# Sparse attention followed by a gated MLP: v on partitions 32 to 95, two raw buffers for k and q, halo rows moved by SyncE, and a new listed order

## The chip, the cores and the metric

The kernel runs on one core of one Trainium2 chip. The metric is the device time of one execution in microseconds. Three runs of the kernel before took 233.87, 235.32 and 235.61 us; their median is 235.32 us. One further execution was profiled; the profile tells the time of every instruction and transfer of that one. The engines are TensorE (PE, with its weight loads PEld), VectorE (DVE), ScalarE (ACT), GpSimd (POOL) and SyncE (SP), which here only starts transfers.

## What is computed

Four batches of eight heads, 768 positions, head size 64, and an MLP from 512 to 2048 and back on the 4 x 768 = 3072 tokens:

```python
# attention, per batch and head: 24 blocks of 32 positions
k_sum = k.reshape(B, H, nb, 32, D).max(axis=3)
v_sum = v.reshape(B, H, nb, 32, D).mean(axis=3)
local = where(abs(i - j) < 16, scale * q @ k.T, -1e9)      # 768 keys, a band of 31
coarse = scale * q @ k_sum.T + log(32)                     # 24 keys
a = softmax(concat([local, coarse], axis=-1))
x = a @ concat([v, v_sum], axis=2)                         # -> [3072, 512] over the heads
# MLP
h = x @ w_in
g = h * clip(h + 3.0, 0.0, 6.0) / 6.0
out = g @ w_out                                            # float32
```

## The kernel before, in words

**Tiles of the attention.** Queries are taken in 12 tiles of 64 (`QB`) per batch, shifted by 16 against the keys. Each tile sees a window of 96 keys (`WIN`: its own block of 64 keys and 32 of the next) and the 24 block maxima, so 120 rows (`KEYS`). `kaug` holds, for each of the four pairs of heads, these 120 key columns of every tile; `vaug` holds the 120 rows of v: window rows on partitions 0 to 95, block sums on 96 to 119, with a column of ones (32 for the sums) that yields the softmax's denominator. A score step (`scores`, names s...) is 24 small matmuls per pair of heads into a pair of PSUM banks, one exponential on ScalarE per half of the tiles (L527), and a multiplication by the 0/1 band on VectorE (L531). A value step (`values`, v...) is 16 or 32 matmuls (L632), a normalisation on VectorE, four transposes (L682) and a copy into x.

**How q, k and v arrive.** All loads from DRAM are started by GpSimd and turn float32 into bfloat16 on the way; they go through one queue in the order of their issue. Batch 0 loads k and q in natural rows (`knat`, `qnat`), and TensorE transposes them. Batches 1 to 3 load k and q raw (`load_raw`): 32 positions on 32 partitions, for one half of the head size and four heads, 3072 rows of 64 bytes; VectorE turns them in 32 x 32 blocks (`turn`, w..., L588 for k and L592 for q). There is one `kraw` and one `qraw`. A load of k takes one transfer per group of 32 partitions (L367), a load of q two, of 16 partitions each (L375), because of the shift by 16. v is loaded in four pieces (L385) onto partitions 0 to 63. The other 32 window rows, those of the next block, are copied inside the core for batch 0 (`halo`); for batches 1 to 3 they are a third load from DRAM (`load_vhalo`, L393, 380 KB), followed by a small move on SyncE for the last tile (L395). The block sums of v are a chain of small matmuls with the indicator `ind` over the 64 rows (L552 and L567); they are copied to the tiles on ScalarE and VectorE, for batches 2 and 3 by SyncE (L575).

**MLP.** The tokens come in eight half batches s = 0 to 7 of 384. Fsc (c = 0 to 3) is a quarter of the first product: per 128 hidden units four matmuls (L700), a ReLU on ScalarE (L705) and a gating step on VectorE that writes g (L707). Gst (t = 0 to 2) is the second product for 128 tokens (four groups of four matmuls of 512 columns, L720), a copy out of PSUM (L432, the line of the helper that records every copy) and a store by SyncE (L730, and L732 for the rows that wrap around the batch). The last tile is cut into two halves of 256 columns.

**What sets the order.** Nothing is reordered at run time. The string `ORDER` lists every operation with its number within its group (F00.3, w21.0, ...), and `:A` or `:D` says which of ScalarE and VectorE takes a copy. `Plan.run` walks the string and assigns buffers: three PSUM banks `h`, one `o`, two pairs `S`, three g, four x. Each engine then executes its own instructions in the order in which they were issued, and waits at one whose inputs are not there; what stands behind it waits too. A load is started in GpSimd's order, once its target is free. At the start some matmuls on constants (`keep`, L803) run between TensorE's first steps.

Of the kernel before, what the change touches and what calls it, by code (L numbers as in the profile page):

```python
# [21 lines left out]
VW = 66  # L22
# [19 lines left out]
F10.3 F12.1 F10.2 F12.2 F10.6 F10.4 F10.9 F10.5 F10.7 F10.8 F11.0 F10.10 F10.11 F11.6 F11.1 F11.9 F11.2 F11.7 F11.8 F11.10
F11.11 F12.6 F12.7 F12.8 F12.9 F12.10 F12.11 w12.0 G01.1 F13.0 F13.1 w13.0 F13.2 w11.0 w13.3 w10.0 w12.3 G01.2 G01.3 F12.3
F13.9 G01.4:A G02.0 G02.1 G02.2 G02.3 F11.3 F13.10 w11.2:A F12.4 F12.5 G02.4:A w12.2:A F13.3 F11.4 F13.4 w10.2:A w13.2:A
w12.4 w11.3 w11.4 w11.1 w11.5:D G00.0 G00.1 s110.0 s110.1 s110.3 w12.1 w13.1 w12.5:D w13.5:A G00.2 G00.3 s120.0 s120.1
s120.3 w13.4 w10.1 F13.5 w10.3 F11.5 w10.4 w10.5:D F13.11 V10.0 V13.0 V11.0 V23.0 V12.0 H1.0 K20.0 K22.0 V20.0 K21.0 Q231.0
K23.0 Q220.0 V22.0 V21.0 Q200.0 Q221.0 Q201.0 Q211.0 Q210.0 Q230.0 s130.0 G00.4:A F13.6 G12.0 s130.3 s130.1 F13.7 G00.5
G01.5 H1.1 G02.5 s120.2 s110.2 s130.2 s100.0 s100.1 F13.8 s100.2 s110.4 s100.3 G12.1 u1.0 u1.1:A u1.3:A u1.5:A G12.2 G12.3
G12.4:A u1.4:D u1.2:D v10.0 s120.4 v10.1 v10.5 v10.6 v10.2 s100.4 u1.7:A u1.6:A u1.9:A G11.0 G11.1 v12.0 v10.3 v10.4:A
u1.8:A v12.1 v12.2 s130.4 G11.2 v10.7 v12.3 v10.8:D G11.3 v12.4:A v13.0 F20.0 F20.3 G11.4:A F20.1 F20.4 v13.5 v13.1 v13.2  # L50
v13.6 F20.9 v13.3 v15.0 F20.10 F20.2 F20.5 F20.11 v15.1 v15.2 F20.6 F21.0 F20.7 F20.8 F21.1 V30.0 V31.0 V32.0 V33.0 F21.2
w21.0 F21.6 G10.0 F21.7 v13.4:A F21.8 F21.3 v15.3 v13.7 F21.9 F22.3 F21.4 F21.5 w20.0 F22.0 G10.1 F21.10 F22.4 v15.4:A
F21.11 F22.1 F22.5 F22.9 F23.0 F22.2 w20.3 F22.10 F22.11 F23.1 w21.2:A v13.8:A F23.2 w22.0 F22.6 u2.0 F22.7 F22.8 w21.3
# [796 lines left out]
```

## Time and profile before

| what | us |
|---|---|
| runs (three), median | 233.87, 235.32, 235.61; 235.32 |
| profiled execution, and its span from first to last instruction | 233.64; 231.9 |
| TensorE busy | 217.3 |
| VectorE busy | 156.7 |
| ScalarE busy | 126.5 |
| GpSimd busy | 72.8 |
| matmuls of the MLP's first product (L700), second product (L720) | 95.0; 82.3 and 10.9 |

The 1.7 us between the profiled execution's time and its span lie before the first and after the last instruction. A row that begins with a line number gives an engine, an operation, its output and its inputs with shapes and how often it occurred, then after a bar the busy time and the mean nanoseconds of one, and after another bar the idle time of the engine just before these instructions with what ended it. In the timeline the first two numbers are the start and the length; the bracket at the end is the idle time before it and what ended that.

### The profile page before, as it was taken

What the parts mean: (1) busy time and instruction counts of PE and PEld (TensorE: products, weight loads), DVE (VectorE), ACT (ScalarE), POOL (GpSimd) and SP (SyncE); (2) the same over time, 40 slices, a digit from 0 to 9 for tenths busy, and PEclk for the clock granted to TensorE, in tenths of its full rate; (3) what the DMA queues carried; (4) which work ended last, traced back from release to release, by engine and by line L of the source; (5) the groups of instructions that cost most, each with busy time, mean ns of one, the idle gap of its engine ahead of it and who ended that gap; (6) DMA issues with size and microseconds to landing.
All of it is one profiled execution on the core that took longest, in us unless ns stands there. A gap on an engine that the chain in (4) does not pass through costs nothing.

```text
span 231.9 us, 5321 instructions
## 1 busy us (share of the span) xinstructions
PE 217.3 (94%) x2175; PEld 121.8 (52%) x2175; DVE 156.7 (68%) x327; ACT 126.5 (55%) x258; POOL 72.8 (31%) x86
## 2 busy tenths in 40 slices
PE   7899699999989997989999889999999999999991
PEld 2365476555445563545565445555555555555560
DVE  2489689789897669889785499945955645454201
ACT  2287567774588854768654535675552543434101
POOL 7994481357754734707741200000000000000000
PEclk9999979999999999999999999999999999999998
DMA  5999999999999999999999990132002030012013
GB/s 76 169 123 182 191 206 196 119 77 87 95 120 176 186 103 86 85 114 146 84 142 89 127 71 0 45 80 84 3 11 85 0 136 3 0 45 90 3 68 114
DMA packets 126585, 22.14 MB, mean 95 GB/s; under 512 B 116960, under 2 KB 123616, under 8 KB 126560
## 3 DMA queue, kind: packets, MB, share of 16 engines
q0 software_dynamic: 117280, 14.81, 217.7%
q1 hardware_dynamic: 9280, 6.98, 12.7%
q8 instruction: 17, 0.28, 0.7%
q14 instruction: 8, 0.07, 0.1%
HBM read 29.60 MB, written 6.29 MB: 155 GB/s over the span
## 4 chain that ended last, share of the span: by engine, by line
PE 58%; DMA 18%; issue 9%; POOL 9%; ACT 2%; DVE 2%; DVEq 0%; POOLq 0%
PE h L700 26%; PE o L720 22%; DMA kraw<-in_k_dram 13%; DMA qnat<-in_q_dram 5%; PE h L720 4%; POOL vaug L385 3%; ACT at L527 2%; PE S L519 1%; PE S L632 1%; POOL qraw L375 1%; POOL qnat L357 1%; PE S L682 1%; POOL knat L346 1%; POOL win L417 1%; POOL kraw L367 1%
## 5 line engine op out<-in xcount | busy, mean ns | idle before, releaser
L700 PE MATMUL h<-x,win 128*128 128x384 bf16 (+1 forms) x536 | 95.0, 321 | 3.1 <-DVE g L707 3.1
L705 ACT ACTIVATE r<-h 128x384 f32<-128x384 f32 x128 | 60.4, 493 | 59.4 <-PE h L700 58.7
L707 DVE SCALAR_TENSOR_TENSOR g<-r,h 128x384 bf16<-128x384 f32 x128 | 67.5, 545 | 33.9 <-ACT r L705 32.1
L720 PE MATMUL o<-wout,g 128*128 128x512 bf16 x336 | 82.3, 379 | 0.2 <-ACT ot L432 0.2
L700 PEld LDWEIGHTS <-win 128*128 128x128 bf16 x536 | 49.9, 99 | 37.5 <-issue 3.6
L720 PEld LDWEIGHTS <-g 128*128 128x128 bf16 x400 | 38.1, 98 | 36.3
L375 POOL DMA_DIRECT2D qraw<-in_q_dram x24 | 21.3, 890 | 29.1 <-issue 10.5
L527 ACT ACTIVATE at<-S 120x768 bf16<-120x768 f32 x32 | 24.8, 812 | 7.1 <-PE S L519 7.1
L367 POOL DMA_DIRECT2D kraw<-in_k_dram x12 | 15.8, 1317 | 13.5 <-issue 12.0
L385 POOL DMA_DIRECT2D vaug<-in_v_dram x16 | 15.1, 949 | 4.8 <-PE h L700 3.1
L592 DVE STREAM_TRANSPOSE qaug<-qraw 128x800 bf16<-128x800 bf16 x12 | 11.8, 998 | 6.2 <-DMA kraw<-in_k_dram 3.3
L667 DVE TENSOR_TENSOR xn<-S,rc 128x512 bf16<-128x512 f32 (+1 forms) x25 | 15.7, 643 | 0.4
L531 DVE TENSOR_TENSOR at<-at,mask 96x768 bf16<-96x768 bf16 x28 | 14.8, 546 | 1.5 <-ACT at L527 1.0
L432 ACT COPY ot<-o 128x512 f32<-128x512 f32 x16 | 9.4, 586 | 11.3 <-PE o L720 10.6
L588 DVE STREAM_TRANSPOSE kaug<-kraw 128x768 bf16<-128x768 bf16 x12 | 11.5, 965 | 2.1 <-DMA kraw<-in_k_dram 2.1
L432 ACT COPY x<-S 128x512 bf16<-128x512 bf16 x19 | 11.0, 587 | 2.5 <-PE S L682 2.1
L519 PEld LDWEIGHTS <-kaug 64*128 64x128 bf16 x384 | 7.0, 96 | 8.2 <-issue 6.3
L605 DVE TENSOR_REDUCE red<-kaug 128x24 bf16<-128x768 bf16 x12 | 11.2, 940 | 0.0
L519 PE MATMUL S<-qaug,kaug 64*128 64x64 bf16 x384 | 9.2, 192 | 2.0 <-ACT at L527 1.2
L803 PE MATMUL o<-idle 128*128 128x512 bf16 x30 | 9.5, 442 | 1.5 <-DVE idle L287 1.5
L720 PE MATMUL h<-wout,g 128*128 128x512 bf16 (+1 forms) x64 | 10.9, 326 | 0.0
L632 PEld LDWEIGHTS <-at 120*64 120x64 bf16 x384 | 7.6, 111 | 5.9 <-issue 4.8
(84 smaller groups left out, 139.3 us busy)
## 6 DMA issues: line engine op xcount, KB each, us to landing
out_dram<-ot SPq DMA_DIRECT2D x19, 256.0 KB
vaug<-in_v_dram POOLq DMA_DIRECT2D x16, 192.0 KB, 10.7
kraw<-in_k_dram POOLq DMA_DIRECT2D x12, 192.0 KB, 14.8
qraw<-in_q_dram POOLq DMA_DIRECT2D x24, 96.0 KB, 11.9
win<-in_moe_w_in_dram POOLq DMA_DIRECT2D x4, 512.0 KB, 11.8
wout<-in_moe_w_out_dram POOLq DMA_DIRECT2D x4, 512.0 KB, 13.5
vaug<-in_v_dram POOLq DMA_DIRECT2D x3, 380.0 KB, 16.2
out_dram<-ot SPq DMA_DIRECT2D x4, 224.0 KB
```

Source lines behind the costliest of these rows:

```text
L367: op("POOL", 0.8, lambda hs=hs, ds=ds, rows=rows: nc.gpsimd.dma_start(out=kraw[rows], in_=k[b, hs].rearrange("h (c r) d -> r (h c) d", r=B ...
L375: nc.gpsimd.dma_start(out=qraw[lo:lo + PAD, 1 - x:1 - x + NP * NB], in_=src[PAD * (1 - x):PAD * (2 - x)])
L385: op("POOL", 0.95, lambda: nc.gpsimd.dma_start(out=o[0:QB, lo:hi, 0:D], in_=rows[:, lo:hi]), w=[("v", b % 2, c)], prio=prio, dma=1.7)
L432: {"ACT": nc.scalar.copy, "DVE": nc.vector.tensor_copy, "POOL": nc.gpsimd.tensor_copy}[eng](o, i)
L519: nc.tensor.matmul(X[p, half].slot[:, j, i * QB:(i + 1) * QB], kaug[p][rows, t], qT[rows, p, t * QB:(t + 1) * QB], start=not masked, stop= ...
L527: op("ACT", act(2 * HALF), lambda a=a, x=x: nc.scalar.activation(a, x.slot[0:KEYS, :, 0:HALF], AF.Exp, scale=scl), r=[x], w=[("at", p, hal ...
L531: op("DVE", dve(2 * HALF, 1.92), lambda m=m, half=half: nc.vector.tensor_tensor(m, m, mask[:, half * HQ:(half + 1) * HQ].unsqueeze(1).to_b ...
L667: nc.vector.tensor_tensor(o, src[..., 0:D], r.unsqueeze(len(r.shape)).to_broadcast(list(o.shape)), op=ALU.mult)
L700: nc.tensor.matmul(h.slot[:, lo * 128:hi * 128], w_in_sb[:, kt, ft * 128:(ft + 1) * 128], xt[s].slot[:, kt, lo * 128:hi * 128], start=(kt ...
L705: op("ACT", act(HALF), lambda: nc.scalar.activation(r.slot[:], h.slot[:, 0:HALF], AF.Relu, bias=0.5, scale=1.0 / 6.0), r=[h], w=[r], prio= ...
L707: op("DVE", dve(HALF), lambda: nc.vector.scalar_tensor_tensor(gt[s].slot[:, ft], r.slot[:], 1.0, h.slot[:, 0:HALF], op0=ALU.min, op1=ALU.m ...
L720: nc.tensor.matmul(o.slot[:, a:z], gt[s].slot[:, ft, ts * 128:(ts + 1) * 128], w_out_sb[:, ft, a:z], start=(ft == 0), stop=(ft == NFT - 1))
```

## The change

- **Place of v.** v is loaded onto partitions 32 to 95. The 32 further window rows lie on partitions 0 to 31 and hold the end of the previous block, so a tile's window is [32 keys of the previous block, its own 64]; the shift by 16 goes the other way, and the last block is the one before the first. Of each batch the second half of the tiles (6 to 11) is now treated first (`low`). Stores follow: the tile that wraps has its 16 wrapped rows first. The row of `vaug` is 80 wide in place of 66.
- **Halo rows.** The third load from DRAM is gone. Batch 1 copies them on ScalarE (five) and VectorE (three); batches 2 and 3 have one SyncE transfer inside the core of 3040 rows each and a small one of 256 rows.
- **Block sums** are taken over 96 rows, with zeros in the indicator and in the 32 rows that the halo will fill (`empty`: four memsets on VectorE at the start for one buffer, four on GpSimd for the other). For batch 0 the sums go to `vf`; for two pairs of heads the values of the first half take the sums' part by separate matmuls on `vf`, in place of two copies to the tiles.
- **Raw k and q** have two buffers each; the second pair shares its space with batch 0's natural k and q. A raw q load is one transfer of 32 partitions like one of k: 12 of them in place of 24. VectorE's block transpose of q is 768 wide in place of 800.
- **Batch 0's q**, second half, is loaded as three pieces of 128 positions (`qwide`), transposed by three matmuls per pair in place of eight.
- **Order.** A new `ORDER`: batch 1's loads come as k, v, q in place of k, q, v; the block maxima may be copied by ScalarE; the list ends with the copy (ScalarE) and store of 256 columns of the tile that is cut in two, in place of a copy of 512 columns and the two stores of a tile that wraps. Matmuls on constants at the start: 35 in place of 47. The constants with which the list was made (`SLOW`, `KRAW`, `LAT`, `room`) change, too.

```diff
@@ class Plan, and the buffers
-KRAW = 2.0
+KRAW = 1.6
...
-    qaug = sb([128, NP, BLK + S], BF16, "qaug")
-    qT = qaug[:, :, BLK:]
-    kraw = sb([128, NP * NB, BLK], BF16, "kraw")
-    qraw = sb([128, NP * NB + 1, BLK], BF16, "qraw")
+    qT = sb([128, NP, PAD + S], BF16, "qT")
+    first = sb([128, 2 * NP * NB, BLK], BF16, "first")
+    kraw, qraw = ([sb([128, NP * NB, BLK], BF16, f"{n}raw"), first[:, i * NP * NB:(i + 1) * NP * NB]] for i, n in enumerate("kq"))
...
-    knat = sb([RP, H, RUN, D], BF16, "knat")
-    qnat = [sb([RP, H, RUN // 2, D], BF16, f"qnat{i}") for i in range(2)]
+    knat, qnat = (first[0:RP].rearrange("p c x -> p (c x)")[:, lo:lo + H * n * D].rearrange("p (h s d) -> p h s d", h=H, s=n)
+                  for lo, n in ((0, RUN), (H * RUN * D, RUN // 2)))
+    qwide = sb([128, NS // 2, d_model], BF16, "qwide")
+    vf = [sb([128, 2, D + 2], BF16, f"vf{c}") for c in range(NP)]
...
-    ind = sb([QB, NQ, 32], BF16, "ind")
+    ind = sb([WIN, NQ, 32], BF16, "ind")
@@ const_ops
+        def empty(eng, i, c):
+            eng.memset(vaug[i][0:BLK, 2 * c:2 * c + 2, :, 0:D].bitcast(F32), 0.0)
+            if i == 0:
+                eng.memset(vf[c][WIN:KEYS, :, D:D + 2], float(BLK))
...
+    def low(x):
+        return (1 - x) * HQ
@@ load_raw
-            for x in range(2):
-                plan.at(f"Q{b}{g}{x}")
-                def go(x=x, hs=hs, ds=ds, lo=BLK * g + PAD * x):
-                    src = q[b, hs].rearrange("h (c r) d -> r (h c) d", r=BLK)[:, :, ds]
-                    nc.gpsimd.dma_start(out=qraw[lo:lo + PAD, 1 - x:1 - x + NP * NB], in_=src[PAD * (1 - x):PAD * (2 - x)])
...
+        for name, src, o in (("K", k, kraw[(b + 1) % 2]), ("Q", q, qraw[(b + 1) % 2])):
+            for g in range(4):
...
+                op("POOL", 1.32, lambda src=src, o=o, hs=hs, ds=ds, rows=rows: nc.gpsimd.dma_start(
+                    out=o[rows], in_=src[b, hs].rearrange("h (c r) d -> r (h c) d", r=BLK)[:, :, ds]),
...
@@ load_v, halo, halos
-        op("POOL", 0.95, lambda: nc.gpsimd.dma_start(out=o[0:QB, lo:hi, 0:D], in_=rows[:, lo:hi]),
+        op("POOL", 0.95, lambda: nc.gpsimd.dma_start(out=o[BLK:WIN, lo:hi, 0:D], in_=rows[:, lo:hi]),
...
-        op("POOL", 0.75, lambda: nc.gpsimd.dma_start(out=o[QB:WIN, 0:n - 1, 0:D], in_=rows[0:WIN - QB, 1:n]),
...
+        def go(eng):
+            copy(eng, o[0:BLK, hs, a:z, 0:D], o[QB:WIN, hs, a - 1:z - 1, 0:D])
+            if x:
+                copy(eng, o[0:BLK, hs, 0, 0:D], o[QB:WIN, hs, NQ - 1, 0:D])
...
+        op("SP", 0.7, lambda: nc.sync.dma_start(out=o[0:BLK, 1:n, 0:D], in_=o[QB:WIN, 0:n - 1, 0:D]),
+           r=[("v", i, c) for c in range(NP)], w=every, free=[("vz", i, c) for c in range(NP)], prio=prio, dma=3.4)
+        op("SP", 0.7, lambda: nc.sync.dma_start(out=end[0:BLK, :, 0, 0:D], in_=end[QB:WIN, :, NQ - 1, 0:D]),
...
@@ turn
-            out=w[:, :, 0:QB].rearrange("p t (n c) -> p t n c", n=2),
-            in_=kraw[:, p * NB:(p + 1) * NB].rearrange("p (t n) c -> p t n c", n=2)),
+            out=w[:, :, BLK:WIN].rearrange("p t (n c) -> p t n c", n=2),
+            in_=kraw[(b + 1) % 2][:, p * NB:(p + 1) * NB].rearrange("p (t n) c -> p t n c", n=2)),
...
-            out=qaug[:, p].rearrange("p (c x) -> p c x", x=BLK), in_=qraw[:, p * NB:(p + 1) * NB + 1]),
+            out=qT[:, p, PAD:PAD + S].rearrange("p (c x) -> p c x", x=BLK), in_=qraw[(b + 1) % 2][:, p * NB:(p + 1) * NB]),
@@ f2
-                nc.sync.dma_start(out=out[b * S + row:b * S + row + n, a:z], in_=ot.slot[0:n, a:z])
-                if n < 128:
-                    nc.sync.dma_start(out=out[b * S:b * S + 128 - n, a:z], in_=ot.slot[n:128, a:z])
+                if n:
+                    nc.sync.dma_start(out=out[(b + 1) * S - n:(b + 1) * S, a:z], in_=ot.slot[0:n, a:z])
+                nc.sync.dma_start(out=out[b * S + row + n:b * S + row + 128, a:z], in_=ot.slot[n:128, a:z])
```

Batch 1's part of the two lists, loads only:

```diff
-K10.0 K11.0 K13.0 K12.0 ... Q121.0 Q101.0 Q110.0 Q100.0 Q120.0 Q131.0 Q130.0 Q111.0 ... V10.0 V13.0 V11.0 V23.0 V12.0 H1.0
+K11.0 K12.0 O3.0 K13.0 z1.1:P K10.0 V12.0 V10.0 V13.0 ... Q10.0 V11.0 z2.1:P Q12.0 Q13.0 Q11.0
```

438 lines of the change are left out of this document (231 added, 207 removed).

## The prediction

> **What bounds the kernel now.** I read the first part of the page (how full each engine is), then its part 4 (the chain that ended last), then stretches of the span, to see where the fullest engine isn't full.
>
> ```profile
> span 231.9 us, 5321 instructions
> PE 217.3 (94%) x2175; PEld 121.8 (52%) x2175; DVE 156.7 (68%) x327; ACT 126.5 (55%) x258; POOL 72.8 (31%) x86
> PE 58%; DMA 18%; issue 9%; POOL 9%; ACT 2%; DVE 2%; DVEq 0%; POOLq 0%
> ```
>
> TensorE is the bound on average, but nearly a fifth of the chain is DMA. The stretches, cut where the batches change (columns: length, then PE, PEld, DVE, ACT, POOL busy with their instructions, granted clock, DMA share, GB/s):
>
> ```profile
> 60.00:80.00 20.00, 18.75 (x300) 10.20 (x299) 15.53 (x34) 17.39 (x31) 11.30 (x11) 1.00 3.75 150
> 80.00:100.00 20.00, 18.41 (x168) 10.47 (x167) 15.77 (x29) 11.35 (x27) 9.73 (x11) 1.00 5.71 96
> 100.00:140.00 40.00, 37.70 (x431) 21.25 (x431) 31.66 (x63) 23.96 (x51) 13.65 (x13) 1.00 3.63 108
> 140.00:227.30 87.30, 87.28 (x663) 47.50 (x661) 47.80 (x97) 38.59 (x81) 0.00 (x0) 1.00 0.13 43
> ```
>
> From 140 us to the end of the matmuls PE is full; nothing but less work helps there. What can be won lies before: 20 − 18.41 = 1.59 us idle between 80 and 100, 40 − 37.70 = 2.30 between 100 and 140, together 3.9. The chain (start, length) and the timeline name the holders:
>
> ```profile
> 14.98 12.10 DMA qnat<-in_q_dram
> 73.13 13.78 DMA kraw<-in_k_dram
> 107.74 10.84 DMA kraw<-in_k_dram
> 126.44 6.13 DMA kraw<-in_k_dram
> 227.37 0.69 DVE ot L432
> ```
> ```profile
> 87.10 0.98 DVE L588 STREAM_TRANSPOSE kaug<-kraw 128x768 bf16<-128x768 bf16 x1 [2.05 <-DMA kraw<-in_k_dram]
> 88.57 1.46 PE L700 MATMUL h<-x,win 128*128 128x384 bf16 x8 [1.37 <-DVE g L707]
> 132.64 1.01 DVE L592 STREAM_TRANSPOSE qaug<-qraw 128x800 bf16<-128x800 bf16 x1 [3.30 <-DMA kraw<-in_k_dram]
> 134.14 2.11 PE L700 MATMUL h<-x,win 128*128 128x384 bf16 x12 [1.73 <-DVE g L707]
> ```
>
> DVE stands in its list at the transpose of a raw k or q that hasn't landed (2.05 us, 3.30 us); the gating step g queued behind it is late, so PE idles 1.37 and 1.73 us. Those two are 3.1 of the 3.9. They have one cause: there is a single raw buffer, so the next batch's load can be issued only when the last transpose of this batch has read it.
>
> **The rates of the loads.** All loads go through GpSimd's software queue, and after the weights it is never empty, so batch 1's time is set by the sum of transfers. Four stretches of the queue, in this order: raw k alone; raw k and q mixed; v; weights; and a fifth of natural q and v at the start:
>
> ```profile
> DMA packets 6748, 0.44 MB, mean 118 GB/s; under 512 B 6747, under 2 KB 6747, under 8 KB 6747
> ...
> DMA packets 6374, 0.40 MB, mean 75 GB/s; under 512 B 6374, under 2 KB 6374, under 8 KB 6374
> ...
> DMA packets 5937, 0.75 MB, mean 117 GB/s; under 512 B 5937, under 2 KB 5937, under 8 KB 5937
> ...
> DMA packets 3455, 2.43 MB, mean 202 GB/s; under 512 B 1176, under 2 KB 3453, under 8 KB 3453
> ...
> DMA packets 840, 0.11 MB, mean 153 GB/s; under 512 B 840, under 2 KB 840, under 8 KB 840
> ```
>
> They last 3.7, 5.4, 6.4, 12 and 0.7 us. A raw load is 3072 packets of 64 B: 6748/3.7 = 1824 a us make 1.7 us a load, 6374/5.4 = 1180 make 2.6. A v load is 1536 packets of 128 B on partitions 0 to 63: 5937/6.4 = 928 a us, 1.66 us. The first rows of the batches need what has to land:
>
> ```profile
> 27.19 1.48 POOL L423 DMA_DIRECT2D wout<-in_moe_w_out_dram  x2 [2.24 <-DMA qnat<-in_q_dram]
> ...
> wout<-in_moe_w_out_dram POOLq DMA_DIRECT2D x1, 512.0 KB, 14.9
> ```
> ```profile
> 61.88 1.01 DVE L592 STREAM_TRANSPOSE qaug<-qraw 128x800 bf16<-128x800 bf16 x1 [1.05 <-DMA qraw<-in_q_dram]
> 63.30 0.52 PE L519 MATMUL S<-qaug,kaug 64*128 64x64 bf16 x24
> 73.48 0.83 PE L632 MATMUL S<-vaug,at 120*64 120x65 bf16 x32
> ```
>
> The second of the two last weight loads is issued at 27.19 + 0.74 = 27.9 and lands 14.9 later, at 42.8. Raw q of batch 1 is complete when its transpose starts, 61.9. The values product of batch 1 (v10.0 in the listed order) starts at 73.48.
>
> **The change part by part.** Durations used (the last number before the second bar is the mean ns):
>
> ```profile
> L527 ACT ACTIVATE at<-S 120x768 bf16<-120x768 f32 x32 | 24.8, 812 | 7.1 <-PE S L519 7.1
> L531 DVE TENSOR_TENSOR at<-at,mask 96x768 bf16<-96x768 bf16 x28 | 14.8, 546 | 1.5 <-ACT at L527 1.0
> L432 ACT COPY ot<-o 128x512 f32<-128x512 f32 x16 | 9.4, 586 | 11.3 <-PE o L720 10.6
> L432 ACT COPY kaug<-kaug 128x352 bf16<-128x352 bf16 (+1 forms) x22 | 6.5, 356 | 0.0
> L432 ACT COPY ot<-h 128x256 f32<-128x256 f32 (+1 forms) x3 | 1.2, 446 | 6.0 <-PE h L720 6.0
> L367 POOL DMA_DIRECT2D kraw<-in_k_dram x12 | 15.8, 1317 | 13.5 <-issue 12.0 <-DMA kraw<-in_k_dram 1.1 <-DVE kaug L608 0.4
> L375 POOL DMA_DIRECT2D qraw<-in_q_dram x24 | 21.3, 890 | 29.1 <-issue 10.5 <-DVE qaug L432 8.3 <-DMA kraw<-in_k_dram 6.6
> L321 POOL MEMSET ind<- 64x384 bf16 x1 | 0.4, 437 | 0.0
> kraw<-in_k_dram POOLq DMA_DIRECT2D x12, 192.0 KB, 14.8
> ```
>
> *Up to v10.0.* The queue order becomes weights, k of batch 1, v of batch 1, then q. The natural q of batch 0 (second half) is now three loads of 1024 rows of 128 B: 3 × 1024 / (840/0.7 = 1200 a us) = 2.6 us, against what I put at 3.0 for the former two of the same bytes: so the weights end at about 42.4. Then 8 raw loads and 4 of v. A raw load: between 1.7 and 2.6; the second figure is from a stretch in which 16-partition q loads ran, and these become 32-partition ones like k's, so I stay nearer to k: 1.9. A v load now writes 64 partitions 32 to 95, which no row shows; bounds are 1.66 (no effect) and 0.97 (196 KB at the 202 GB/s of the weights, which go to all 128 partitions); I take 1.28, the rate of the fifth stretch, whose packets are equally long and go to 64 to 96 partitions. Raw q complete: 42.4 + 8 × 1.9 + 4 × 1.28 = 62.7.
>
> From there to v10.0: in the old run 63.30 + 0.52 − 61.88 = 1.9 us to the first scores' end. Then ScalarE has seven exponentials, one output copy, the two copies of a halo of k and a relu (0.49, like other relus of its shape) between them, and DVE the last mask: 7 × 0.812 + 0.586 + 2 × 0.356 + 0.49 + 0.546 = 8.0. v10.0 at 62.7 + 1.9 + 8.0 = 72.6, against 73.48: **−0.9**. That v10.0 was late for another reason before, the row of the copied halo below, which goes. What precedes (earlier first F, 12 fewer idle matmuls, sums from `vf`, zeroing on DVE) lies under this wait for the queue and is set at nothing; without that wait I count, by the listed order and the matmul groups in it, v10.0 at about 70.7. The eight halo copies of batch 1 (5 on ScalarE) read v, which lands before q: the wait for q covers them. GpSimd's own time falls (12 × 1.317 against 24 × 0.890 us), and its four memsets of 768 words, some 0.9 us each by L321's rate, stand before loads that take 14.8 us to land after their issue: the queue covers them.
>
> *From v10.0 to the last matmul.* The list holds the same matmuls in both from here. With a second raw buffer, batch 2's and 3's loads are issued a stage earlier, and the stalls of 2.05 and 3.30 us go; 3.1 of the 3.9 us of idle with them. What is late next is DVE itself (31.66 of 40 us busy), short hand-overs that I leave at 1.0 us. **−2.9**; bounds 0 and −3.9.
>
> The halo rows of v for batches 2 and 3 leave that queue too. Rows on SyncE:
>
> ```profile
> L575 SPq DMA_DIRECT2D vaug<-vs x16: 778/802/1951, 97.6 to 154.6; - x16
> L395 SPq DMA_DIRECT2D vaug<-vaug x3: 644/657/747, 72.9 to 126.3; - x3
> 228.69 0.44 SPq L732 DMA_DIRECT2D out_dram<-ot  x1
> ```
>
> L395 moves 256 rows in 0.657 us, L575 288 rows in 0.802, the last store 16 in 0.44. The new move is of 3040 rows: by the slope 16 to 256 it takes 0.44 + 3024 × 0.0009 = 3.2 us, in proportion to L395 7.8, by the slope 256 to 288 13. I take 7.8. Ahead of it and queued behind it on SyncE stand four spreads of block sums each (L575, 0.8); v20.0 waits for all of them, and by the list 18.7 us of PE work lie between. 3.2 + 7.8 + 3.2 and some 2 us to land are 16.2: covered, so nothing in the sum. At 13 it is 21.4, 2.7 us late, and later by whatever the transfer takes beyond 2.
>
> *Tail.* The old end is a 512-column copy on DVE (0.69) and a second store of 16 rows (0.44) behind the first. The list now ends with the half tile: a 256-column copy (0.446) and one store. **−0.7**.
>
> Sum: 231.9 − 0.9 − 2.9 − 0.7 = 227.4 us of span. The profiled execution took 233.64, 1.74 more than its span, so 229.1; it lies between the runs (233.87 to 235.61, median 235.32) and below them by 0.1 to 0.8%, so the median may come out half a us above my number. I keep 229.5.
>
> [...]
>
> **The rivals.**
> 1. *The supply is no longer late.* If v takes 0.97 and raw loads 1.7, q is complete at 42.4 + 13.6 + 3.9 = 59.9, scores and exponentials end at 69.8 and PE's own work sets v10.0, 70.7: −2.8 in place of −0.9, 225.5 + 1.74 = 227.2. [...] Against: ScalarE, 17.39 of 20 us busy there, gets five more copies. [...]
> 2. *Slower: v ahead of q, and raw loads stay slow.* At 2.6 and 1.66 q is complete at 42.4 + 20.8 + 6.6 = 69.8, v10.0 at 79.7, +6.3; batch 2's twelve loads take 27.4 more, to 97, no earlier than now, so the −2.9 goes as well: 231.9 + 6.3 − 0.7 + 1.74 = 239.2. It decides from about 2.55 us a raw load (then over 1% slower). For it: the 75 GB/s stretch was raw loads of both kinds. Against: k alone ran at 118.
> 3. *SyncE held by its moves.* At 13 us, v20.0 is 2.7 us late; if the transfer also takes 5 us, as three v loads of 1536 rows do, 5.7: 232 to 235. For it: the steeper slope. Against: it is drawn through two points close together.
> 4. *The new list brings its own stalls*, as large as those removed (three buffers h, one o as before): the −2.9 becomes 0 to +1: 232.5 to 233.5. For it: DVE 79% busy between 100 and 140. This is also the case in which the second buffer doesn't do what it says, since other readers (kaug, still single) hold the transposes.
>
> **How the numbers follow.** Forecast 0.38 (227 to 231.3), rival 1 0.24, rival 2 0.16, rival 3 0.11, rival 4 0.11. About 1% (233.0 to 237.7 around the median) is what a measurement of this kernel can tell from no change. Faster: forecast, rival 1 and a little of rival 4, 0.62; slower: rival 2 and the worse half of rival 3, 0.21; the same 0.17. The range leaves out rival 2's 239 and the tip of rival 1: 225 to 237.5.
>
> **What would show it.** Right: no idle of DVE before stream transposes that ends on raw k or q after 75 us; v10.0 at 70 to 74; the v stretch of batch 1 above 130 GB/s; PE idle between v10.0 and the last matmul under 1.5 us; the chain without the two longest raw-k links. Wrong: raw loads above 2.4 us each, scores of batch 1 after 67 us, a SyncE instruction of over 10 us with v20.0 waiting on it, or PE idle before g in new places.

## The result, and the profile after

The changed kernel takes 227.81 us (median of four runs, 227.11 to 229.01) against 234.59 us (233.54 to 235.61): ratio 0.9717, 95% interval 0.9648 to 0.9785. The forecast was 229.5. Some executions take over 1.5% longer than the fastest of the same kernel; the ratios here and below leave them out and compare with the kernel before as it ran beside each kernel. The profiled execution took 228.21 us, its span is 226.5 us, 5.4 less than before; the forecast sum for it was 227.4.

The head of the page of the changed kernel, then its stretches from 60 us on (columns as before: length, PE, PEld, DVE, ACT, POOL busy, granted clock, DMA share, GB/s):

```profile
span 226.5 us, 5318 instructions
PE 216.4 (96%) x2167; PEld 120.8 (53%) x2167; DVE 158.1 (70%) x329; ACT 132.9 (59%) x274; POOL 65.3 (29%) x75
PE 68%; DMA 12%; POOL 11%; issue 5%; DVE 2%; ACT 1%; POOLq 0%
```
```profile
60.00:73.40 13.40, 11.10 (x133) 5.47 (x130) 11.50 (x24) 10.71 (x19) 10.14 (x9) 0.87 5.14 135
73.40:80.00 6.60, 6.46 (x97) 3.77 (x97) 6.05 (x13) 5.69 (x9) 3.57 (x3) 1.00 2.65 160
80.00:100.00 20.00, 20.00 (x235) 11.59 (x234) 16.73 (x33) 14.43 (x33) 11.58 (x10) 1.00 3.56 147
100.00:140.00 40.00, 40.00 (x424) 22.28 (x422) 33.70 (x67) 23.73 (x54) 0.00 (x0) 1.00 0.52 63
140.00:222.50 82.50, 82.47 (x626) 45.20 (x618) 42.64 (x88) 36.88 (x75) 0.00 (x0) 1.00 0.14 47
```

The idle time of 1.59 and 2.30 us between 80 and 140 is gone to the last digit, and raw k no longer appears in the chain (the row of raw q there is that of batch 1). What is left lies ahead of batch 1's values: 13.40 − 11.10 = 2.3 us idle, at a mean clock of 0.87. The chain there and at the end, and TensorE's waits in its timeline (the first row is the first F, the first matmul of the MLP's first product; that of the kernel before stands by itself at the end):

```profile
52.18 10.43 DMA qraw<-in_q_dram
62.64 0.99 DVE qT L627
222.51 0.37 ACT ot L463
```
```profile
25.43 0.38 PE L742 MATMUL h<-x,win 128*128 128x128 bf16 x4
63.67 0.35 PE L557 MATMUL S<-qT,kaug 64*128 64x64 bf16 x12 [0.80 <-DVE qT L627]
64.27 0.35 PE L557 MATMUL S<-qT,kaug 64*128 64x64 bf16 x12 [0.24 <-DVE qT L463]
65.52 0.35 PE L557 MATMUL S<-qT,kaug 64*128 64x64 bf16 x12 [0.90 <-ACT at L566]
66.22 0.35 PE L557 MATMUL S<-qT,kaug 64*128 64x64 bf16 x12 [0.35 <-DVE vaug L463]
73.40 1.02 PE L671 MATMUL S<-vaug,at 120*64 120x65 bf16 x32
```
```profile
30.30 2.45 PE L700 MATMUL h<-x,win 128*128 128x128 bf16 x20
```

Cut at three events, the two profiled executions and those of the experiments below read as follows ("values" is the start of batch 1's values, "last" the end of the last matmul; "to values" and "to last" are differences of the unrounded times; the last column is the landing of the last load):

| kernel | first F | to values | values of batch 1 | to last | last | raw q of batch 1 complete |
|---|---|---|---|---|---|---|
| before | 30.3 | 43.2 | 73.5 | 153.8 | 227.3 | 61.9 |
| changed | 25.4 | 48.0 | 73.4 | 149.1 | 222.5 | 62.6 |
| changed, once more | 25.3 | 45.6 | 71.0 | 149.5 | 220.5 | 61.6 |
| shorter queue (`w2_one`) | 27.8 | 47.0 | 74.8 | 148.9 | 223.8 | 53.4 |
| late q of batch 0 (`qwide_late`) | 28.7 | 50.5 | 79.3 | 148.9 | 228.2 | 63.3 |
| one raw buffer (`one_raw`) | 28.7 | 45.7 | 74.4 | 158.6 | 233.0 | 61.9 |
| before, two raw buffers | 32.6 | 43.9 | 76.5 | 149.5 | 226.0 | 63.1 |
| before, two raw buffers, once more | 29.2 | 43.9 | 73.1 | 155.6 | 228.7 | 61.8 |
| before, halo rows by SyncE | 29.3 | 47.4 | 76.7 | 152.3 | 228.9 | 63.9 |

So in the pair of profiles the change gains 4.7 us behind batch 1's values and 0.6 at the tail (226.5 − 222.5 = 4.0 against 231.9 − 227.3 = 4.6), and ahead of the values nothing: the first F starts 4.9 us earlier, and the way from it to the values is 4.8 us longer.

### The profile page after: what moved, and what is told of

The parts are those of the page before. It is cut to its first block, busy times and chain, and to the rows that moved or that the text cites. A ratio compares the mean times of both kernels' runs of the same rounds, so it can differ in the third digit from the quotient of the medians.

```text
span 226.5 us, 5318 instructions
## 1 busy us (share of the span) xinstructions
PE 216.4 (96%) x2167; PEld 120.8 (53%) x2167; DVE 158.1 (70%) x329; ACT 132.9 (59%) x274; POOL 65.3 (29%) x75
## 4 chain that ended last, share of the span: by engine, by line
PE 68%; DMA 12%; POOL 11%; issue 5%; DVE 2%; ACT 1%; POOLq 0%
PE h L742 28%; PE o L762 28%; DMA wout<-in_moe_w_out_dram 7%; DMA qraw<-in_q_dram 5%; PE h L762 5%; POOL vaug L414 3%; PE S L671 3%; PE S L557 2%; PE S L724 2%; POOL qraw L403 2%; POOL win L448 1%; POOL qwide L394 1%; POOL first L374 1%; PE S L605 1%; DVE qT L627 1%
## 5 line engine op out<-in xcount | busy, mean ns | idle before, releaser
L747 ACT ACTIVATE r<-h 128x384 f32<-128x384 f32 x128 | 61.4, 491 | 51.0 <-PE h L742 48.9
L762 PE MATMUL o<-wout,g 128*128 128x512 bf16 x336 | 83.7, 384 | 0.0
L463 ACT COPY ot<-o 128x512 f32<-128x512 f32 x18 | 10.6, 588 | 8.4 <-PE o L762 8.4
L463 ACT COPY x<-S 128x512 bf16<-128x512 bf16 x18 | 10.3, 585 | 3.9 <-PE S L724 2.8
L403 POOL DMA_DIRECT2D qraw<-in_q_dram x8 | 10.5, 1313 | 7.3 <-issue 5.2
L403 POOL DMA_DIRECT2D kraw<-in_k_dram x8 | 10.5, 1318 | 4.6 <-issue 2.9
L557 PE MATMUL S<-qT,kaug 64*128 64x64 bf16 x384 | 9.6, 194 | 2.3 <-ACT at L566 0.9
L848 PE MATMUL o<-idle 128*128 128x512 bf16 x20 | 7.7, 472 | 1.6 <-DVE idle L300 1.6
L671 PE MATMUL S<-vaug,at 120*64 120x65 bf16 x352 | 8.4, 197 | 0.1
L724 PEld LDWEIGHTS <-xn 128*128 128x128 bf16 x96 | 6.9, 98 | 2.8
```

Source lines behind the costliest of these rows:

```text
L403: op("POOL", 1.32, lambda src=src, o=o, hs=hs, ds=ds, rows=rows: nc.gpsimd.dma_start(out=o[rows], in_=src[b, hs].rearrange("h (c r) d -> r ...
L463: {"ACT": nc.scalar.copy, "DVE": nc.vector.tensor_copy, "POOL": nc.gpsimd.tensor_copy}[eng](o, i)
L557: nc.tensor.matmul(X[p, half].slot[:, j, i * QB:(i + 1) * QB], kaug[p][rows, t], qT[rows, p, t * QB:(t + 1) * QB], start=not masked, stop= ...
L671: nc.tensor.matmul(y, a[:, cols], vaug[b % 2][0:KEYS, h, t, 0:D + 1], start=True, stop=True)
L747: op("ACT", act(HALF), lambda: nc.scalar.activation(r.slot[:], h.slot[:, 0:HALF], AF.Relu, bias=0.5, scale=1.0 / 6.0), r=[h], w=[r], prio= ...
L762: nc.tensor.matmul(o.slot[:, a:z], gt[s].slot[:, ft, ts * 128:(ts + 1) * 128], w_out_sb[:, ft, a:z], start=(ft == 0), stop=(ft == NFT - 1))
```

## The experiments

My theory after the prediction: raw q's landing sets the start of batch 1's values, and one raw buffer was the cause of both stalls behind it. The rivals: TensorE's own work from the first F on sets the values; and the stalls came from the length of the queue (the halo loads in it), not from the buffer.

### Does the queue set the start of batch 1's values?

`w2_one` leaves three quarters of w_out unloaded:

```diff
-    for c in range(4):
+    for c in range(1):
         load_w2(c, -34 + c)
...
-nc.tensor.matmul(o.slot[:, a:z], ..., w_out_sb[:, ft, a:z],
+nc.tensor.matmul(o.slot[:, a:z], ..., w_out_sb[:, ft - 4 * max(ft // 4 - 0, 0), a:z],
```

> The changed kernel without the loads of the last three quarters of w_out: the second product uses the first quarter four times, so its output is another one; the work of the engines stays. The queue is shorter by 3 x 2.53 = 7.6 us before batch 1's raw q. If raw q's landing sets the start of batch 1's values: q lands near 55, and the values start at 69 to 70.7 us, where the engines hold them; 2.5 to 4 us less in all. If ScalarE and VectorE hold them already: they start at 72.5 to 73.5 and the time stays within 1 us of the changed kernel.

Measured: 229.44 us (one run). Raw q is complete at 53.4, 8 to 9 us earlier than in the two traces of the changed kernel, and the values come no earlier. (The first F is 2.4 us later, with the same loads ahead of it; in this execution TensorE was slower for a while before it: two matmuls of L550 took 0.75 us at 13.68, against 0.43 at 11.80.) Its first F and its values:

```profile
27.84 0.38 PE L744 MATMUL h<-x,win 128*128 128x128 bf16 x4
74.84 0.88 PE L673 MATMUL S<-vaug,at 120*64 120x65 bf16 x32
```

The values start 47.0 us after the first F, as in the changed kernel (48.0 and 45.6) and in the three other traces with its first part (48.2 in `rates`, 47.0 in `rates2`, 46.0 in `halo_dram_list`), although raw q lay there for 11 us before VectorE transposed it (53.4 to 64.4). At its present length the queue doesn't set them; raw q merely lands at about the time at which the engines get to it. A longer queue would be felt: in the changed kernel's first trace VectorE did wait for raw q, if for only 0.24 us, and in the kernel before with halo rows by SyncE, where raw q is complete at 63.9, it waited 3.88 us and the values came 47.4 us after the first F, in place of 43.2. The theory that the engines' own work from the first F on sets the values is tested from the other end, by a later first F with an unchanged landing of raw q: `qwide_late` moves batch 0's loads of the second half of q in the list,

```diff
-... V01.0 ... Q01w2.0 c.6 V02.0 V03.0 ... Q01w1.0 I0.0 Q01w0.0 ... I1.0 O0.0 I2.0
+... V01.0 ... c.6 V02.0 V03.0 ... I0.0 ... I1.0 O0.0 Q01w2.0 Q01w1.0 Q01w0.0 I2.0
```

> The changed kernel with the three loads of batch 0's second half of q behind two of w_in and one of w_out in the queue, in place of among them; nothing else moves, and batch 1's loads end as before. TensorE's first F stands in its list behind a transpose of that q, so it starts 2 to 3 us later, at 27.5 to 28.5 in place of 25.4. Queue theory (the prediction's: batch 1's raw q sets the start of its values, what lies before is covered): values at 71 to 73.4 as now, time within 0.7 us of the changed kernel. Start theory (formed on the run with the shorter queue: TensorE's own work from the first F on sets it): values at 73.5 to 76, 2 to 3 us more.

Measured: 233.3 us (median of ten, 230.46 to 234.66), ratio to the kernel before 0.9875 (0.9815 to 0.9935); the changed kernel, measured again, has 226.76 and 0.9676 (below). Two stretches at the start and three ahead of the values, then three rows of TensorE, two of VectorE ahead of its transpose of q, and the same two in the changed kernel once more:

```profile
26.00:28.00 2.00, 0.00 (x0) 0.00 (x0) 0.23 (x1) 0.45 (x3) 2.00 (x4) 1.00 1.44 200
28.00:30.00 2.00, 1.96 (x19) 1.99 (x20) 1.02 (x3) 0.17 (x1) 2.00 (x2) 0.51 1.25 207
...
68.00:70.00 2.00, 0.41 (x16) 0.39 (x18) 1.97 (x5) 0.04 (x1) 1.42 (x2) 1.00 6.23 108
70.00:72.00 2.00, 0.74 (x32) 0.60 (x34) 1.94 (x5) 1.67 (x3) 1.31 (x1) 1.00 6.17 111
72.00:74.00 2.00, 2.00 (x18) 0.94 (x16) 1.97 (x4) 1.98 (x4) 1.78 (x2) 0.60 6.08 110
```
```profile
28.73 0.63 PE L744 MATMUL h<-x,win 128*128 128x128 bf16 x4
69.17 0.35 PE L559 MATMUL S<-qT,kaug 64*128 64x64 bf16 x12 [2.08 <-DVE qT L629]
79.25 0.88 PE L673 MATMUL S<-vaug,at 120*64 120x65 bf16 x32
```
```profile
65.51 0.96 DVE L465 COPY kaug<-red 128x288 bf16<-128x288 bf16 x1
67.21 1.02 DVE L465 COPY kaug<-red 128x288 bf16<-128x288 bf16 x2
```
```profile
60.08 0.23 DVE L463 COPY kaug<-red 128x288 bf16<-128x288 bf16 x1
61.09 0.37 DVE L463 COPY kaug<-red 128x288 bf16<-128x288 bf16 x2
```

Raw q is complete at 63.3, about as before the edit, and the values come at 79.3, 6 to 8 us later. 3.3 us are the later first F. The way from it to the values is 4.9 us longer than in the trace with the full clock (50.5 against 45.6): 2.5 of them are busy time, in which the clock falls twice, after each of two waits (0.51 from 28 to 30 us; 0.60 and 0.55 from 72 to 76), and 2.4 are idle time (4.15 against 1.75 us). Most of these 2.4 us is the wait of 2.08 us for VectorE's transpose of q. Raw q had been there since 63.3; VectorE was late (68.15), since its copies ahead took longer: these two rows 1.4 us more together than in the other trace, and a copy of halo rows 1.25 in place of 0.42. They end at 66.47 and 68.23, within 0.2 us of the ends of two of GpSimd's load instructions (66.44 and 68.11; see the last section). So the start, which the forecast had set at nothing, matters: 3.3 us of it put the values 6 to 8 us later, and the time is 4 to 6 us longer (by the ratios 0.9875 against 0.9676 and 0.9717, by the medians 233.3 against 226.76 and 227.81). How much of the time is the start alone and how much the waits that came with it, one trace doesn't tell. The changed kernel itself, once more:

> The changed kernel once more, beside the kernel before and the next kernels. If the stretch up to batch 1's values is set by how fast the queue happens to run, its start moves by a us or more between executions (73.40 and 72.33 us so far in two kernels with the same first part); if it is set by the engines, it stays within 0.3 us. Ratio 0.965 to 0.98 either way.

Measured: 226.76 us (median of four, 226.15 to 228.19), ratio 0.9676 (0.9592 to 0.9759). The values start 2.4 us earlier than in the first trace, with the first F at the same time. The stretches around the scores, first trace and then this one:

```profile
64.00:66.00 2.00, 0.73 (x26) 0.64 (x25) 1.97 (x5) 1.34 (x2) 1.54 (x2) 1.00 6.61 108
66.00:68.00 2.00, 1.78 (x19) 0.94 (x19) 1.97 (x3) 2.00 (x4) 1.32 (x1) 0.81 6.63 110
68.00:70.00 2.00, 2.00 (x28) 0.89 (x27) 1.97 (x7) 0.88 (x4) 1.40 (x2) 0.50 5.31 142
70.00:72.00 2.00, 2.00 (x10) 0.71 (x10) 0.98 (x3) 1.69 (x3) 1.96 (x2) 0.84 2.06 227
```
```profile
64.00:66.00 2.00, 1.14 (x28) 0.78 (x28) 1.94 (x5) 2.00 (x4) 1.47 (x2) 1.00 5.46 109
66.00:68.00 2.00, 2.00 (x32) 1.01 (x31) 1.97 (x6) 1.98 (x5) 1.51 (x2) 1.00 5.49 126
68.00:70.00 2.00, 2.00 (x32) 0.99 (x30) 1.78 (x6) 1.78 (x4) 1.45 (x2) 1.00 2.75 206
```

After the waits between the scores the clock fell in the first trace (0.81, 0.50, 0.84 of full) and not in this one. That makes the 2.4 us: by the three rows quoted with the steps of the prediction below, 1.4 of them are longer matmuls and 0.9 waits.

### What removed the stalls behind the values?

The kernel before with two raw buffers, its list unchanged:

```diff
-    kraw = sb([128, NP * NB, BLK], BF16, "kraw")
-    qraw = sb([128, NP * NB + 1, BLK], BF16, "qraw")
+    kraw = [sb([128, NP * NB, BLK], BF16, f"kraw{i}") for i in range(2)]
+    qraw = [sb([128, NP * NB + 1, BLK], BF16, f"qraw{i}") for i in range(2)]
...
```

`load_raw` and `turn` take `kraw[b % 2]` and `qraw[b % 2]` throughout.

> The kernel before with two raw buffers for k and q and nothing else changed, its listed order kept. Prediction's theory (one buffer is the one cause of both stalls): the waits of VectorE for raw k at 87 us (2.05) and 132 us (3.30) go, about 3 us faster, ratio about 0.987. Queue theory, formed on the old trace (raw k of batch 2 was issued from 61 us on without waiting for a transpose and was late because the halo load of 4.5 us and others stood ahead; only raw q of batch 3 waited 8.3 us for its buffer): the stall at 87 us stays at 1.5 to 2.5 us, that at 132 us falls, 1 to 2 us faster, ratio 0.991 to 0.997.

> The kernel before with two raw buffers once more, for a second trace of it. Idle of TensorE after batch 1's values again under 0.5 us (4.2 in the kernel before). If the 2.3 us by which its first F was late last time (32.6 against 30.3) are chance, the first F starts at 29 to 31 and the span is 227 to 229 us; if they come with the buffers, it starts after 32 again, and the span is 230 to 231.

Measured: 233.39 us (ratio 1.007, 1.002 to 1.013), and 233.43 us (0.989, 0.982 to 0.996): about 1%, and of either sign. In the first trace all idle time behind the values is gone, but there they start 3 us later than in the kernel before, so that batch 2's loads had 3 us more to land. In the second (an execution of 235.23 us, of 230.25 to 236.36 for this kernel) the values start at 73.1 and batch 2's waits are back; in the kernel before they are 1.37 and 0.79:

```profile
87.92 1.46 PE L700 MATMUL h<-x,win 128*128 128x384 bf16 x8 [1.22 <-DVE g L707]
102.20 0.53 PE L519 MATMUL S<-qaug,kaug 64*128 64x64 bf16 x24 [2.94 <-DVE qaug L592]
```

Batch 3's wait at 132 us is in neither. But all idle time behind the values is as long as in the kernel before (155.64 − 151.38 = 4.3 us against 4.1), since the wait for batch 2's q has grown; that fits the time, which hardly moves. So the second buffer cures batch 3 alone; batch 2's raw k and q were late because of what stood ahead of them in the queue. The opposite edit, the changed kernel with one raw buffer (`kraw[0]`, `qraw[0]` for every batch; batch 2's and 3's loads behind the last transposes that read it):

> The changed kernel with one raw buffer for k and one for q; the loads of k and q of batches 2 and 3 stand in GpSimd's list behind the last transposes that read the buffer, all else as listed. If the second buffer is what took the idle time after batch 1's values away: VectorE waits at the transposes of batch 2's q for some 4 us and at batch 3's for 5 to 15 us (its list asks for them earlier than the old one did), TensorE idles for 4 to 15 us after 73 us; 2 to 6% slower than the changed kernel. If the halo loads were what held the queue: under 2 us of idle, within 1%.

Measured: 239.3 us (two runs), ratio 1.020 (1.004 to 1.037), 5% over the changed kernel. No wait in batch 2, and one in batch 3:

```profile
119.45 2.72 PE L744 MATMUL h<-x,win 128*128 128x384 bf16 x8 [8.20 <-DVE g L751]
```

This again says: in the changed list the buffer belongs to batch 3. For batch 2 the landings of its last raw k and q say the same (us):

| kernel | buffers | raw k of batch 2 | raw q of batch 2 |
|---|---|---|---|
| before | one | 86.9 | 99.4 |
| before, two raw buffers (twice) | two | 86.1; 86.3 | 98.1; 101.0 |
| changed (twice) | two | 73.8; 72.5 | 79.6; 78.2 |
| changed, one raw buffer | one | 70.8 | 82.1 |

The number of buffers moves them by at most 4 us, the changed list with its loads by 13 us and more. Next, the halo rows. The kernel before with its halo loads of batches 2 and 3 replaced by SyncE moves (for b > 1),

```diff
-        op("POOL", 0.75, lambda: nc.gpsimd.dma_start(out=o[QB:WIN, 0:n - 1, 0:D], in_=rows[0:WIN - QB, 1:n]),
+        op("SP", 0.75, lambda: nc.sync.dma_start(out=o[QB:WIN, 0:n - 1, 0:D], in_=o[0:WIN - QB, 1:n, 0:D]),
```

> The kernel before with the halo rows of v for batches 2 and 3 moved inside the core by SyncE, in place of the two loads of 380 KB from DRAM; batch 1 keeps its load, all else and the listed order stay. Prediction's theory: the raw buffer is what holds, so about 0 to 1 us. Queue theory: the two loads took 5.5 and 6.0 us of the queue ahead of raw q and k of batch 3, so batch 3's raw loads land 5 to 10 us earlier, the stall at 132 us goes, the one at 87 us stays; 1.5 to 2.5 us faster, ratio 0.989 to 0.994. If SyncE is held for 8 us or more by each move, the values of batch 2 are late by up to 3 us instead.

and the changed kernel with its moves replaced by loads behind all others:

```diff
-        op("SP", 0.7, lambda: nc.sync.dma_start(out=o[0:BLK, 1:n, 0:D], in_=o[QB:WIN, 0:n - 1, 0:D]),
+        op("POOL", 0.75, lambda: nc.gpsimd.dma_start(out=o[0:BLK, 1:n, 0:D], in_=rows[BLK:QB, 0:n - 1]),
```

> The changed kernel with the halo rows of batches 2 and 3 loaded from DRAM through the software queue again (380 KB each), issued after all other loads since they must follow the block sums. In the changed kernel the queue is empty from 110 us on. Both theories: the halo of batch 2 lands at about 115 us, plus 1 to 2 us for the small move behind it, against 112.6 us at which the values of batch 2 start now: 3 to 5 us of idle on TensorE there, 1 to 2% slower than the changed kernel; batch 3's is hidden. If the move on SyncE was the dearer one, no change.

Measured: the first 235.23 us (ratio 1.016, 1.002 to 1.031), no gain in time; its way from the values to the last matmul is 152.3, 1.5 less, and the wait at 132 us is gone, so it too cures batch 3; batch 2's waits stay (1.28 and 1.42 us), and ahead of the values it loses by the late raw q described above. The second 227.11 us (226.13 to 227.7; ratio 0.9805, 0.9713 to 0.9897), the same as the changed kernel; I had expected 1 to 2% more. The halo of batch 2 landed at 108.5 instead of 115. What the move costs on SyncE stands in its timeline, changed kernel first, then with the loads:

```profile
100.18 0.70 SPq L437 DMA_DIRECT2D vaug<-vaug  x1
100.97 10.86 SPq L578 DMA_DIRECT2D vaug<-vs  x6
```
```profile
100.00 6.95 SPq L578 DMA_DIRECT2D vaug<-vs  x6
```

The move of 3040 rows is issued in 0.70 us; the six spreads behind it take 10.86 in place of 6.95. In the changed kernel once more the six take 9.86. With the move, raw k of batch 3 is complete at 109.3 (once more 106.9), without it at 104.6; 1.5 us of the difference to 109.3 were there before the move was issued (the load that landed at 98.0 there landed at 96.5 here). So the row that I scaled to 7.8 us was of the wrong instruction: the move holds the next ones, by 3 to 4 us, and the raw loads beside it land later.

### The rate of the v loads

A first kernel with extra loads in the quiet part (`rates`, 229.75 us) told nothing of rates: nothing held its loads back, so they were issued from 97 us on, right behind batch 3's and beside SyncE's transfers.

> The changed kernel with 27 extra loads in the stretch from about 121 us on, in which its queue is empty; nothing reads what they bring. In groups, each waiting for the one before: three v loads of 1536 packets to partitions 0 to 63 with a row of 66, three to 32 to 95 with 66, three to 0 to 63 with 80, three to 32 to 95 with 80, four raw loads on 32 partitions, eight of half size on 16 partitions, three v loads to 64 to 127. [...] Packet theory: all v loads take the same, about 1.3 to 1.7. [...] Raw loads: 1.7 to 2.1 us on 32 partitions; two half loads on 16 partitions together 2.1 to 2.6. The time stays within 1% of the changed kernel, since TensorE waits for none of them.

`rates2` writes them into `vaug[0]`, which is free only after batch 2's values, and there they run alone:

> The changed kernel with 32 extra loads once the values of batch 2 are done, in an otherwise empty queue; nothing reads what they bring. Four v loads each to partitions 0 to 63 with a row of 80, 32 to 95 with 80, 0 to 63 with 66, 32 to 95 with 66, 64 to 127 with 80; then four raw loads on 32 partitions and eight half loads on 16. [...] Estimate of the prediction: 1.28 and 1.66. Row theory: the width 80 (rows that begin at multiples of 32 bytes) is what helps, 1.3 against 1.6, whatever the partitions. Raw loads 1.7 to 2.1 us; two half loads together 0.3 to 0.6 more.

Measured (226.34 us): four loads each to partitions 0 to 63 with a row of 80, to 32 to 95 with 80, and to 0 to 63 with 66:

```profile
DMA packets 5949, 0.77 MB, mean 152 GB/s; under 512 B 5948, under 2 KB 5948, under 8 KB 5948
...
DMA packets 5940, 0.75 MB, mean 145 GB/s; under 512 B 5940, under 2 KB 5940, under 8 KB 5940
...
DMA packets 4267, 0.54 MB, mean 130 GB/s; under 512 B 4267, under 2 KB 4267, under 8 KB 4267
```

The stretches last 5.06, 5.19 and 4.18 us: 1.31, 1.34 and 1.50 us a load of 1536 packets. In these loads the place on partitions made no difference (1.31 against 1.34 us); the row of 80 did, by an eighth (1.31 against 1.50). The groups after these ran beside SyncE's transfers and aren't read.

### Filling the wait

Two tries to use the 2.3 us ahead of the values. `fill_h` moves G00's copy and G12's groups forward, puts G11 into a bank of h and moves the SyncE move of batch 2 forward; `fill2` mends its order. The order of the changed kernel and that of `fill2`:

```diff
-G00.3 ... h110.0:A ... s100.0 s100.3 s100.1 G00.4:A s110.0 ... F13.3 G12.0 s120.0 ... s120.2 G12.1 G12.2 s130.0 ... G12.3 G12.4:A ... v10.0 ... G11.0 G11.1
+G00.3 ... G00.4:A G00.5 h110.0:A ... s100.0 s100.3 s100.1 G12.0 s110.0 ... F13.3 G12.1 s120.0 ... s120.2 G12.2 s130.0 G11.0 G11.1 ... v10.0 G12.3 G12.4:A ...
```

> The changed kernel with another order between raw q's landing and batch 1's values: the copy of G00 out of PSUM ahead of a halo copy on ScalarE, G12's groups moved into TensorE's waits between the scores, G11 in a bank of h so that it can start before G12 has been copied; and the large SyncE move of batch 2 directly behind the block sums' matmuls. TensorE idles 2.6 us there now and its granted clock falls to 0.72 for 5 us after it. If idle time there is lost time: 1.5 to 3 us less than the changed kernel (ratio to the kernel before 0.955 to 0.965), the clock stays above 0.9. Rival: the chain of seven exponentials on ScalarE sets the start of batch 1's values and TensorE then waits behind them: within 0.7 us of the changed kernel.

> As the run with the other order between raw q and batch 1's values, mended by its trace: there G11 and G12 stood in TensorE's list ahead of the values when these were ready (1.5 us). Now the first two groups of G11 fill the wait before the values, and G12's last, the rest of G11 and two groups of G10 follow them. If idle time before the values is lost time: 1 to 2 us less than the changed kernel (ratio to the kernel before 0.955 to 0.965). If VectorE and ScalarE behind it set the pace: within 0.7 us of the changed kernel, with new waits of TensorE between 73 and 80 us.

Measured: 228.9 us (228.08 to 229.84) and 228.02 us (227.67 to 228.29; ratio 0.9718, 0.9617 to 0.9819). Neither beats the changed kernel. In `fill2` the work done early is missing later:

```profile
72.65 0.70 PE L673 MATMUL S<-vaug,at 120*64 120x65 bf16 x32
85.19 0.81 PE L744 MATMUL h<-x,win 128*128 128x384 bf16 x4 [0.43 <-DVE g L751]
86.50 1.46 PE L744 MATMUL h<-x,win 128*128 128x384 bf16 x8 [0.27 <-DVE g L751]
```

The values don't come earlier: the last exponentials ahead of them on ScalarE end at 72.28, which I take to be what sets them; and from 78 us on TensorE waits for steps of VectorE and ScalarE. I have no version that is faster than the changed kernel beyond the spread.

## Why the prediction was right in sum, and where its steps failed

- **The sum.** 227.4 us of span were forecast and 226.5 measured; the terms were −0.9, −2.9 and −0.7, and measured −0.1, −4.7 and −0.6. That the sum came so close is in part luck: nearly nothing came of the first term, and the second was 1.8 us larger.
- **"What precedes ... lies under this wait for the queue and is set at nothing" failed.** Raw q was complete at 62.6 where I had 62.7, but that number hardly bound (0.24 us): 8 to 9 us less of queue gave nothing (`w2_one`), a first F 3.3 us later put the values 6 to 8 us later (`qwide_late`). What bound is the engines' work from TensorE's first F on (45.33 of 47.97 us TensorE is busy). In the kernel before the wait for the queue was there, 1.05 us in the row that I quoted; but what lies under it in the old kernel need not do so in the new one. Two terms that I hadn't priced cancel in the profiled pair: the first F 4.9 us earlier, and 4.8 us more from there to the values. The stretch from the first F to the values, in the kernel before, the changed one, and the changed one once more:

```profile
30.30:73.48 43.18, 41.94 (x460) 24.29 (x456) 37.91 (x74) 30.68 (x62) 22.92 (x23) 0.98 4.51 131
```
```profile
25.43:73.40 47.97, 45.33 (x484) 25.56 (x484) 41.21 (x84) 37.56 (x75) 27.92 (x25) 0.96 3.85 147
```
```profile
25.33:70.97 45.64, 43.89 (x483) 24.98 (x483) 40.66 (x84) 37.73 (x75) 27.38 (x25) 1.00 3.31 151
```

Of the 4.8 us, 1.4 are idle time (47.97 − 45.33 = 2.64 against 43.18 − 41.94 = 1.24). 3.4 are busy time: 2.0 of it also in the execution with the full clock (43.89 − 41.94, 23 matmuls more, while the whole kernel has 8 fewer: work that lay ahead of the first F), and 1.4 the halved clock (45.33 − 43.89). The kernel before has a low clock at the start of its stretch, too (0.61 from 30.3 to 32.3 us; 0.98 on the mean).
- **Rates.** Raw loads were put at 1.9 us and were 2.1 on the mean of batch 1's eight; v at 1.28 and was 1.38; the weights took 1.9 us less than I had (to 40.5, without the two loads of k ahead of the last of them). The errors cancelled in 62.7, which is luck: 40.5 + 16.6 + 5.5 against 42.4 + 15.2 + 5.1. That a half load on 16 partitions is the slower form, my reason for 1.9, isn't shown by any run.
- **From raw q to the values** I had 9.9 us and measured 10.8: the clock, which I had left at 1.00 although the rows of the old kernel that I quoted begin at 60 us, behind its own fall. With the full clock it was 9.4 (changed kernel once more).
- **"They have one cause: there is a single raw buffer" failed for batch 2.** With two buffers its waits stay (1.22 and 2.94 us), with one in the changed kernel they stay away. Its loads were late by the queue: batch 1's last load lands at 72.8 in the kernel before and at 62.6 in the changed one. Of these 10.2 us the halo load is 2.9, the weights 2.3, the eight raw loads 2.5 (19.1 against 16.6) and v 2.5 (8.0, with one load of batch 2 among them, against 5.5). No run takes these away one at a time. Batch 3's wait goes with the second buffer, or with the halo loads gone. What was right: nothing took the place of these stalls, and not 2.9 but all 3.9 us of idle behind the values went (4.06 to 0.14), so rival 4 (the new list brings its own stalls) was not met. The remaining 0.8 of the 4.7 is busy time of the same 1369 matmuls (149.74 against 148.93); its cause stays open.
- **Tail:** the copy and the one store as forecast, 0.1 us short.
- **Rival 1 (the supply is no longer late)** describes the mechanism best (the engines' own work sets the values), and gave 227.2; its 70.7 for the values came out near in the changed kernel once more (71.0, at the full clock). But its term for v, 0.97 us a load on partitions 32 to 95, is shown by no run: `rates2` has 1.34 us there (145 GB/s) and 1.31 on 0 to 63 (152 GB/s), and batch 1's v took 1.38 a load. Its raw loads, put at 1.7 us, took 2.1.
- **Rival 2 (raw loads stay slow, v ahead of q)** was not met: raw loads took 2.1 us and v 1.38. Its threshold of 2.55 us is wrong by its own terms: it keeps the −2.9 that the rival gives up, and without it 1% is reached at 2.2. No run has a slower queue in the changed kernel; the late raw q in the kernel before with halo rows by SyncE (3.88 us of waiting) says that it would have been felt.
- **Rival 3 (SyncE held)**: held by 3 to 4 us, not 8 to 13, and covered. The last raw k of batch 3 lands 4.6 and 3.9 us behind the load before it with the move, and 1.9 with a load in its place behind all others. That the move needs some 2 us to land was my estimate, and no run shows it; in the changed kernel TensorE starts batch 2's values at 112.49 us without a wait.

## What to carry to other kernels

Before a stage is called bound by its transfers, ask how long the input lies there before it is used: shorten the queue and see whether anything moves. An event that happens to fall together with the landing of its input looks bound by both. And price the start: what stands ahead of the first full work of the bound engine in its own list is paid once in idle time and can be paid again in its clock (in `qwide_late` a first F that is 3.3 us late, then a clock of 0.51 from 28 to 30 us).

## What was not expected of the hardware

**The clock fell after short waits.** In the first trace of the changed kernel TensorE was busy 1.20 + 0.73 of the 4 us from 62 to 66, with no wait longer than 0.90, and its clock then stood at 0.50 for 3.41 us (67.24 to 70.65); in the second it was busy 1.19 + 1.14 and the clock stayed. In the 3.41 us ahead of the slow stretch TensorE was busy for 1.92. What decides between the two executions isn't shown. Of the 2.4 us between them the clock makes 1.4 (45.33 − 43.89 us busy).

**Copies on VectorE that end with GpSimd's instruction.** The copy of 16 columns of q took 0.16 us on the mean in the kernel before; in the changed one, beside GpSimd's starts of raw loads:

```profile
62.93 1.31 POOL L403 DMA_DIRECT2D first<-in_k_dram  x1 [0.64 <-issue]
63.66 0.55 DVE L463 COPY qT<-qT 128x16 bf16<-128x16 bf16 x1
64.56 1.31 POOL L403 DMA_DIRECT2D first<-in_k_dram  x1 [0.32 <-issue]
65.07 0.77 DVE L463 COPY qT<-qT 128x16 bf16<-128x16 bf16 x1
```

Both copies end with the load instruction (64.21 and 64.24, 65.84 and 65.87). They cost 0.4 to 0.6 us a time on the way from raw q to the scores (0.55 and 0.77 against 0.16). Not every copy beside such a load is longer: the next of this form, at 68.13, took 0.17 us beside the load instruction of 68.01 to 69.32. In `qwide_late` three longer copies end so (the two above, and the copy of halo rows at 63.21, with the load instruction at 63.15), and VectorE comes to raw q 4.9 us after its landing (68.15 against 63.3).
